# Numerators of a linear attention as 56-by-32 products, features padded to 64, row maxima gathered in columns

## The chip, the cores and the metric

The kernel runs on one core of one Trainium2 chip. The time is the device time of one execution in microseconds (us); where several executions were timed, it is their median. A profile is one further execution, recorded instruction by instruction; its span runs from its first to its last instruction, and its own device time is a little longer than the span.

The engines are named as in the profile: PE is TensorE's matrix products and PEld its weight loads, DVE is VectorE, ACT is ScalarE, POOL is GpSimd, SP is SyncE, which issues all of the kernel's DMAs here. PSUM is the memory that products are written to, in banks of 512 float32 per partition. L507 is line 507 of the kernel.

## What is computed

Two attentions over the same 2048 tokens of 448 features, 16 heads of 28, mixed by a gate per token. The first (A) is linear: queries and keys go through a small matrix per head, then through two softmaxes over 28 values each, and only sums over the tokens are needed. The second (B) is an ordinary softmax attention.

```python
def _A_ref(x, wqkv, w_phi, wo):
    q, k, v = ...                                   # 16 heads of 28
    pq = jnp.einsum("bhsd,hdf->bhsf", q, w_phi)
    pk = jnp.einsum("bhsd,hdf->bhsf", k, w_phi)
    phi_q = jnp.concatenate([_softmax(pq, axis=-1), _softmax(-pq, axis=-1)], axis=-1)
    phi_k = jnp.concatenate([_softmax(pk, axis=-1), _softmax(-pk, axis=-1)], axis=-1)
    kv = jnp.einsum("bhsf,bhsd->bhfd", phi_k, v)    # 56 x 28 per head
    z  = jnp.einsum("bhsf->bhf", phi_k)
    num = jnp.einsum("bhqf,bhfd->bhqd", phi_q, kv)
    den = jnp.einsum("bhqf,bhf->bhq", phi_q, z)[..., None] + 1e-6
    return (num / den) @ wo                         # heads side by side

def _B_ref(x, wqkv, wo):
    scores = jnp.einsum("bhqd,bhkd->bhqk", q, k) * scale
    return (_softmax(scores, axis=-1) @ v) @ wo     # heads side by side

g = _sigmoid((x * gate_w).sum(-1, keepdims=True))
out = g * _A_ref(...) + (1 - g) * _B_ref(...)
```

All inputs and the output are float32.

## The kernel before, in words

The order of the instructions on PE, DVE, ACT and POOL is the order of the program text, written out by hand; the DMAs on SP are ordered by the framework's scheduler, each waiting for its semaphores, and one that waits holds back those behind it.

**Stages.** First the projections to B's queries and keys are computed and kept in DRAM (`proj_qk`). Then comes a loop of 43 rounds (line 681) in which a round i handles key tile t = i and query tile q = i - 16 of attention A, 128 tokens each. Then follow B's values (`value_b`), and from line 1104 on B's attention: 256 steps s, sixteen key tiles for each of 16 groups gq (4 groups of heads by 4 blocks of 512 queries). In a step, `scores` computes 4 heads' scores (line 830), `exps_of` their exponentials on ACT (line 838), and `values` two steps later the products with the values (line 975).

**Features of A.** The weights of A's queries are multiplied by the per-head matrix beforehand (`fold`). For a tile, a product of 448 columns gives pq; `features1` copies it out of PSUM on ACT, takes maximum and minimum per head on DVE (lines 417, 418), subtracts them on POOL (line 420) and on POOL or DVE (line 422, by the argument `eng`), and puts the exponential on ACT's list (line 424). `features2`, called for the tile before, sums (line 431), inverts and scales on POOL (line 433). A tile of features is 16 heads by 2 softmaxes by 28, 896 values per token; it rotates through four buffers, which also hold the last four loads of x before the loop (`load_last`).

**Keys.** `kv_add` adds the products of key features and values to the bank pkv: head 4g + j has its 32 rows (28 values, a one for the sum z, padding) at partitions 32j and its 56 columns at 56g. At round q = 2 `kv_copy` copies pkv out with each 56 columns doubled, at q = 3 `kv_out` turns the copy with four products and multiplies it with a mask, so that KV holds eight blocks of 112 rows by 64 columns, each with two heads on its diagonal.

**Numerators.** `turn` turns a tile's features with eight products, two heads (112 columns) in each, and ACT copies them to fT, 112 partitions by 8 pairs of heads by 256 tokens (two tiles). `numer` multiplies eight times a block of KV with a pair's fT:

```python
for g in range(NG):
    for hh in range(2):
        n = 2 * g + hh
        nc.tensor.matmul(pn[g // 2][64 * hh:64 * hh + 64, g % 2 * 256:g % 2 * 256 + 256],
                         KV[:, n, :], fT_of[tb][:, n, :], start=True, stop=True,
                         tile_position=(0, 64 * hh))
```

`tile_position` gives the row and the column of the array at which the product's weights lie. `normalize1` copies the two banks pn out on ACT and sends the denominators, one row of each 32, by DMA through DRAM to all rows; `normalize2` to `normalize4` divide and split the result into two parts for the output projection `out_a` (line 518), which takes three products for each of four groups of heads. A tile runs through subtraction, turning, numerators and output projection in different rounds (y = q - 1 counts them, lines 727 to 783).

**Row maxima of B.** The exponentials need each query's largest score beforehand, so all scores are computed a second time ahead, with one product and a maximum each. In the first part `mx_unit` does it for groups 0 to 4: four products of 28 rows at four row positions into four banks (line 260), a Relu on ACT and a pass on DVE (line 265); the next unit needs the four banks back. From group 5 on, three such products (line 288) go with every step of B's attention, each reduced on DVE (line 295). The partial maxima lie in `part`. When a group is complete, `mx_reduce` puts a function on the list `fin`, which reduces them to 16 columns of `red` (line 229) and turns `red` in 32-by-32 blocks into a tile `nm` (line 234), of which there are seven buffers. `load_nm` later copies nm's rows into the stack of the group's queries (line 816), four DMAs of 2 KB, where the score products subtract them; the stack alternates between two buffers. In the loop of steps, `load_q(gq + 1)` is called at step 5 of group gq, `load_nm(gq + 1)` at step 12 (at step 14 for group 14), and that of group 15 as soon as its maxima are there.

Of the kernel before, what the change touches and what calls it, by code (L numbers as in the profile page):

```python
# [17 lines left out]
P = 128  # L18
# [18 lines left out]
def f32(ap):  # L37
    return ap.bitcast(F32)
# [3 lines left out]
def gated_mix_kernel(ctx, tc, xT, wqkB, wvB, wvA, wkAT, wqAT, phi, woA, woB,  # L42
# [180 lines left out]
    def mx_reduce(gq):  # L223

        col = 64 * gq
        n = 2 if gq < GM else 4

        def reduce():
            nc.vector.tensor_reduce(
                red.rearrange("p (t c) -> p t c", t=4)[:, :, :4],  # L230
                part[:, col:col + 16 * n].rearrange("p (k t h) -> p t h k", t=4, h=4),
                AX.X, ALU.max)
            nm_of[gq] = nm = mxp.tile([P, 128], F32, tag="nm", name=f"nm{gq}", bufs=7)
            nc.vector.transpose(nm, f32(red))

        mxs["fin"].append(reduce)

# [80 lines left out]

    def load_last(b):

        raw = bd.tile([P, H, 2, DH], F32, tag="feat", name=f"xraw3_{b}", bufs=4)
        raw = raw.rearrange("p h s f -> p (h s f)")[:, :512]
        nc.sync.dma_start(raw, xT[:, b, 1536:])
        return raw

# [43 lines left out]
    def normalize1(pool, pn, nm, n):  # L369

# [41 lines left out]
    def features1(pp, nm, eng):  # L412

        pc = bd.tile([P, H, DH], F32, tag="pc", name=f"pc{nm}", bufs=2)
        nc.scalar.copy(pc, pp[:, :D].rearrange("p (h f) -> p h f", f=DH))
        ext = bd.tile([P, 2, H], F32, tag="ext", name=f"ext{nm}", bufs=3)
        nc.vector.tensor_reduce(ext[:, 0, :], pc, AX.X, ALU.max)
        nc.vector.tensor_reduce(ext[:, 1, :], pc, AX.X, ALU.min)
        f = bd.tile([P, H, 2, DH], F32, tag="feat", name=f"feat{nm}", bufs=4)
        nc.gpsimd.tensor_sub(f[:, :, 0, :], pc,  # L420
                             ext[:, 0, :].unsqueeze(2).to_broadcast([P, H, DH]))
        eng.tensor_sub(f[:, :, 1, :],
                             ext[:, 1, :].unsqueeze(2).to_broadcast([P, H, DH]), pc)
        exps.append(lambda: nc.scalar.activation(f, f, AF.Exp))
        return f

    def features2(f, nm):

        f2 = f.rearrange("p h s f -> p (h s) f")
        sm = bd.tile([P, 2 * H], F32, tag="fsum", name=f"fsum{nm}", bufs=3)  # L430
        nc.vector.tensor_reduce(sm, f2, AX.X, ALU.add)
        nc.vector.reciprocal(sm, sm)
        nc.gpsimd.tensor_mul(f2, f2, sm.unsqueeze(2).to_broadcast([P, 2 * H, DH]))
        return f.rearrange("p h s f -> p (h s f)")

    exps = []

# [6 lines left out]
    def kv_add(t):  # L444

        pf, pvv = fk.pop(t), va.pop(t)
        for g in range(NG):
            for j in range(4):
                h = 4 * g + j
                nc.tensor.matmul(pkv[32 * j:32 * j + 32, g * 56:(g + 1) * 56], pvv[:, h, :],  # L450
                                 pf[:, h * 56:(h + 1) * 56], start=t == 0 and g == 0,
                                 stop=t == NT - 1, tile_position=(0, 32 * j),
                                 skip_group_check=True)

# [14 lines left out]
    def kv_copy():  # L469

        kvT = ta.tile([P, D], F32, tag="ga", name="kvT", bufs=2)
        nc.scalar.copy(
            kvT.rearrange("p (g i f) -> p g i f", i=2, f=56),
            pkv[:, :224].rearrange("p (g f) -> p g f", f=56).unsqueeze(2).to_broadcast([P, NG, 2, 56]))
        return kvT

    def kv_out(kvT):

        pt = ps_s("pkvT")
        for g in range(NG):  # L480
            nc.tensor.transpose(pt[:112, g * P:(g + 1) * P], kvT[:, g * 112:(g + 1) * 112], ident)
        nc.vector.tensor_mul(KV, pt[:112].rearrange("p (n c) -> p n c", c=64),
                             mask_s.unsqueeze(1).to_broadcast([112, 8, 64]))

    def turn(u):

        tb, tl = divmod(u, 2)
        if tl == 0:
            fT_of[tb] = ta.tile([112, 8, 256], F32, tag="fT", name=f"fT{tb}", bufs=1)
        f = fq.pop(u)  # L490
        cut = (0, 4, 8) if u < NT - 2 else (0, 3, 6, 8)
        pt = [ps_s(f"pft{u}_{i}") for i in cut[:-1]]
        for a, b, p in zip(cut, cut[1:], pt):
            for n in range(a, b):
                nc.tensor.transpose(p[:112, (n - a) * P:(n - a + 1) * P],  # L495
                                    f[:, n * 112:(n + 1) * 112], ident)
        for a, b, p in zip(cut, cut[1:], pt):
            nc.scalar.copy(fT_of[tb][:, a:b, tl * P:(tl + 1) * P],
                           p[:112, :(b - a) * P].rearrange("p (n q) -> p n q", q=P))

    def numer(tb):

        pn = [ps_s(f"pn{tb}_{i}") for i in range(2)]
        for g in range(NG):
            for hh in range(2):
                n = 2 * g + hh
                nc.tensor.matmul(pn[g // 2][64 * hh:64 * hh + 64, g % 2 * 256:g % 2 * 256 + 256],  # L507
                                 KV[:, n, :], fT_of[tb][:, n, :], start=True, stop=True,
                                 tile_position=(0, 64 * hh))
        num[tb] = normalize1(ta, pn, f"a{tb}", 2)  # L510

    po_of = {}
# [168 lines left out]
    for i in range(2 * NT + 11):  # L681
# [14 lines left out]
        if q == 2:  # L696
# [4 lines left out]
            KV = ta.tile([112, 8, 64], F32, name="KV")  # L701
# [509 lines left out]
```

## Time and profile before

| | us |
|---|---|
| median of 3 runs | 989.11 |
| the runs | 989.56, 989.11, 986.35 |
| the profiled execution's own time | 986.75 |
| its span | 985.0 |
| A's numerators, first to last start | 204.8 to 284.7 |
| B's attention, 256 steps | from about 356 on |

The page of the profile gives each engine's busy time, the chain of work that ended last with its shares by engine and line, and groups of instructions as "line engine operation out<-in shapes xcount | busy, mean ns of one | idle time before them and what ended it". Three further views are used: the chain in order of time and the timeline (start, duration, engine, what, count), and busy times by stretches. A product's end in the trace is modelled, so a duration of a product holds some 0.16 us in which the next has already begun; starts are better for counting.

### The profile page before, as it was taken

To read this page: it belongs to the slowest core of one execution; us is meant where nothing else is said; L and a number is where in the kernel's file an instruction comes from. 1 tells how busy PE (TensorE), PEld (TensorE's weight loads), DVE (VectorE), ACT (ScalarE), POOL (GpSimd) and SP (SyncE) were. 2 spreads that over 40 slices of the span, in tenths; PEclk is the share of its full clock that TensorE was granted. 3 is DMA by queue.
4 is the path that set the end of the run, shared out by engine and by line. 5 is a ranking of instruction groups with operands and counts; after the bars stand their busy time and mean duration, and the time that the engine had idled before them with its cause. 6 is when DMAs were issued, how large, how long until landed. Compare 5 with 4: busy or idle time off the path is not lost.

```text
span 985.0 us, 22282 instructions
## 1 busy us (share of the span) xinstructions
PE 979.2 (99%) x8392; PEld 607.2 (62%) x8392; DVE 728.5 (74%) x1335; ACT 752.9 (76%) x1442; POOL 234.8 (24%) x224
## 2 busy tenths in 40 slices
PE   9999999999999999999999999999999999999998
PEld 8877877887777665555555555555555555555555
DVE  5566767899766678888888888888888888885112
ACT  4455655577775689988988988988888898897561
POOL 1135535578734710031011001011001011000010
PEclk9999999999999999999999999999999999999999
DMA  9873010013233233121132121122231223000451
GB/s 304 310 253 116 33 54 32 36 37 98 79 103 112 90 114 127 37 58 46 65 89 73 35 61 48 57 82 71 61 83 50 60 58 84 22 20 31 132 159 57
DMA packets 56140, 84.47 MB, mean 86 GB/s; under 512 B 17217, under 2 KB 23985, under 8 KB 56033
## 3 DMA queue, kind: packets, MB, share of 16 engines
q1 hardware_dynamic: 56032, 83.06, 27.3%
q8 instruction: 66, 1.08, 0.5%
q14 instruction: 42, 0.34, 0.1%
HBM read 54.86 MB, written 27.78 MB: 84 GB/s over the span
## 4 chain that ended last, share of the span: by engine, by line
PE 95%; DVE 3%; issue 1%; ACT 0%; POOL 0%; DVEq 0%; POOLq 0%; ACTq 0%
PE g L830 29%; PE pv L975 26%; PE pqk L109 6%; PE poa L109 4%; PE pk L127 4%; PE pva L127 4%; PE g L288 3%; PE pmd L260 3%; PE pob L109 3%; PE pvb L127 2%; PE pvb L109 2%; PE pq L109 2%; PE pn L507 1%; PE pqk L608 1%; PE pft L495 1%
## 5 line engine op out<-in xcount | busy, mean ns | idle before, releaser
L838 ACT ACTIVATE p<-g 128x512 f32<-128x512 f32 x1020 | 526.1, 607 | 83.9 <-PE g L830 83.1
L295 DVE TENSOR_REDUCE part<-g 128x1 f32<-128x512 f32 x704 | 442.3, 684 | 84.4 <-PE g L288 80.4
L830 PEld LDWEIGHTS g<-qst,kst 32*128 32x128 f32 x3060 | 221.2, 183 | 212.1 <-DVE part L295 194.6
L830 PE MATMUL g<-qst,kst 32*128 32x512 f32 x3060 | 337.9, 420 | 0.1
L975 PE MATMUL pv<-p,vb 128*32 128x512 f32 x2048 | 273.0, 605 | 0.0
L288 PE MATMUL g<-kc,qc 28*128 28x512 f32 x704 | 233.3, 495 | 0.0
L394 POOL TENSOR_TENSOR oUb<-oUb,rsb 128x512 f32<-128x512 f32 x15 | 19.3, 1286 | 490.5 <-DMA rsb<-rdb 458.4
L265 DVE CUSTOM_DVE_ANT_0 rl<-pmb,rl 128x512 f32<-128x512 f32 x160 | 103.2, 682 | 44.0 <-ACT rl L264 44.0
L264 ACT ACTIVATE rl<-pmd 128x512 f32<-128x512 f32 x160 | 87.3, 601 | 31.2 <-PE pmb L260 30.0
L288 PEld LDWEIGHTS g<-kc,qc 28*128 28x128 f32 x704 | 86.5, 182 | 0.2
L975 PEld LDWEIGHTS pv<-p,vb 128*32 128x32 f32 x2048 | 40.7, 108 | 65.9 <-issue 64.6
L109 PE MATMUL pqk<-XH,wB 128*128 128x512 f32 x192 | 59.1, 397 | 0.0
L986 DVE SCALAR_TENSOR_TENSOR acc<-pob,gate,acc 128x448 f32<-128x448 f32 x12 | 8.2, 684 | 54.7 <-PE pob L109 54.7
L546 ACT CAST ev<-pqk 128x512 fp32r<-128x512 f32 x28 | 16.0, 589 | 39.5 <-PE pqk L109 23.0
L109 PE MATMUL poa<-woA_s,oTa 128*128 128x448 f32 x192 | 43.5, 375 | 0.0
L260 PE MATMUL pmb<-kp,qp 28*128 28x512 f32 x160 | 42.1, 496 | 0.4
L547 DVE TENSOR_TENSOR ev<-pqk,ev 128x512 fp32r<-128x512 f32 x28 | 19.0, 690 | 30.9 <-ACT ev L546 30.8
L109 PEld LDWEIGHTS pqk<-XH,wB 128*128 128x128 f32 x192 | 35.5, 188 | 8.5 <-issue 1.5
L260 PE MATMUL pmd<-kp,qp 28*128 28x512 f32 x160 | 39.9, 494 | 0.0
L127 PE MATMUL pk<-wkA_s,XH 128*128 128x448 f32 x128 | 39.4, 382 | 0.0
L109 PEld LDWEIGHTS poa<-woA_s,oTa 128*128 128x128 f32 x192 | 35.0, 189 | 6.3 <-issue 2.9
L127 PE MATMUL pva<-wvA_s,XH 128*128 128x450 f32 x128 | 37.8, 372 | 0.0
(154 smaller groups left out, 1089.2 us busy)
## 6 DMA issues: line engine op xcount, KB each, us to landing
qkd<-ev SPq DMA_DIRECT2D x28, 512.0 KB
qst<-qkd SPq DMA_DIRECT2D x64, 112.0 KB
kst<-qkd SPq DMA_DIRECT2D x64, 112.0 KB
od<-oTb SPq DMA_DIRECT2D x48, 112.0 KB
rsa<-rda SPq DMA_DIRECT2D x8, 512.0 KB
oL<-od SPq DMA_DIRECT2D x8, 512.0 KB
rsb<-rdb SPq DMA_DIRECT2D x15, 256.0 KB
gad<-ga SPq DMA_DIRECT2D x16, 224.0 KB
```

What stands on the lines that cost most here:

```text
L109: nc.tensor.matmul(dst, l, r, start=i == 0, stop=i == len(todo) - 1)
L127: nc.tensor.matmul(dst[:, :n], l, r, start=i == 0, stop=i == len(todo) - 1, skip_group_check=True)
L260: nc.tensor.matmul(pm[j], qc[js, qt * P:(qt + 1) * P], kc[js, :], start=True, stop=True, tile_position=(32 * i, 0))
L264: nc.scalar.activation(rl, pm[i], AF.Relu)
L265: nc.vector.tensor_tensor_reduce(rl, pm[2 + i], rl, 1.0, LOWEST, ALU.add, ALU.max, part[:, col + i:col + i + 1])
L288: nc.tensor.matmul(pm, mxs[("qc", gq)][js, qt * P:(qt + 1) * P], mxs[("kc", gq // NQ, kb)][js, :], start=True, stop=True, tile_position=(3 ...
L295: nc.vector.tensor_reduce(part[:, col:col + 1], pm, AX.X, ALU.max)
L394: (nc.gpsimd if n == 1 else nc.vector).tensor_mul(oU, oU, rs)
L547: nc.vector.tensor_sub(e[:, 1, :], pq, f32(e[:, 0, :]))
L830: nc.tensor.matmul(st[j], kst_of[(gq // NQ, kt // 4)][js, k, (kt % 4) * P:(kt % 4 + 1) * P], qst_of[gq][js, q, :], start=n == 0, stop=n == ...
L838: nc.scalar.activation(p, st[j], AF.Exp, scale=SCALE)
L975: nc.tensor.matmul(pv[32 * j:32 * j + 32, :], vb[kt // 8][:, kt % 8, 4 * g + j, :], pt[j], start=kt == 0, stop=kt == NT - 1, tile_position ...
```

## The change

It touches two parts. In attention A, a head's features take 64 columns instead of 56, the last eight unused; the order of the query heads in a tile is permuted, by writing the folded weights `wqA_s` in another order, so that the pair turned together is head 4(2k) + j and head 4(2k + 1) + j. Two turned heads then lie at partitions 0 to 55 and 64 to 119 of fT. KV becomes two blocks of 128 by 128 without zero blocks, so the mask is no longer applied; `kv_copy` no longer doubles columns and clears the padding, `kv_out` turns two blocks instead of four and copies. The numerators are sixteen products of 56 rows by 32 columns, at two row positions and four column positions, the two row positions into two banks; each still has 256 moving columns. Their results lie in another order, which `out_a` follows. The subtraction of line 422 goes to POOL for q = 2. The padding of the four feature buffers is cleared on POOL, for the loads of x that use them first.

For the row maxima, the reduction of group gq writes columns 4(gq % 8) to 4(gq % 8) + 3 of each 32 of `red`; the turn is done in `load_nm`, into one of two buffers, and the rows that belong to the group are loaded from it.

```diff
         n = 2 if gq < GM else 4
+        r = 4 * (gq % 8)
 
         def reduce():
             nc.vector.tensor_reduce(
-                red.rearrange("p (t c) -> p t c", t=4)[:, :, :4],
+                red.rearrange("p (t c) -> p t c", t=4)[:, :, r:r + 4],
                 part[:, col:col + 16 * n].rearrange("p (k t h) -> p t h k", t=4, h=4),
                 AX.X, ALU.max)
-            nm_of[gq] = nm = mxp.tile([P, 128], F32, tag="nm", name=f"nm{gq}", bufs=7)
-            nc.vector.transpose(nm, f32(red))
+            nm_of[gq] = True
...
-        raw = bd.tile([P, H, 2, DH], F32, tag="feat", name=f"xraw3_{b}", bufs=4)
-        raw = raw.rearrange("p h s f -> p (h s f)")[:, :512]
+        raw = bd.tile([P, H, 64], F32, tag="feat", name=f"xraw3_{b}", bufs=4)
+        nc.gpsimd.memset(raw[:, 8:, 56:], 0.0)
+        raw = raw.rearrange("p h f -> p (h f)")[:, :512]
...
-        nc.scalar.copy(dst[:, 0, bs, gs], pw3)
-        nc.vector.tensor_sub(dst[:, 1, bs, gs], pw3, f32(dst[:, 0, bs, gs]))
+        hi, lo = dst[:, 0, bs, gs], dst[:, 1, bs, gs]
+        if nm == "q":
+            pw3 = pw3.rearrange("p b (j f) -> p b j f", f=DH)
+            hi, lo = [dst[:, i, bs, g // 2 * 224:g // 2 * 224 + 224].rearrange(
+                "p b (j e f) -> p b j e f", e=2, f=DH)[:, :, :, g % 2, :] for i in range(2)]
+        nc.scalar.copy(hi, pw3)
+        nc.vector.tensor_sub(lo, pw3, f32(hi))
...
-        f = bd.tile([P, H, 2, DH], F32, tag="feat", name=f"feat{nm}", bufs=4)
+        fw = bd.tile([P, H, 64], F32, tag="feat", name=f"feat{nm}", bufs=4)
+        f = fw[:, :, :2 * DH].rearrange("p h (s f) -> p h s f", s=2)
...
-        exps.append(lambda: nc.scalar.activation(f, f, AF.Exp))
+        fe = fw[:, :, :2 * DH]
+        exps.append(lambda: nc.scalar.activation(fe, fe, AF.Exp))
...
-        nc.gpsimd.tensor_mul(f2, f2, sm.unsqueeze(2).to_broadcast([P, 2 * H, DH]))
+        nc.gpsimd.tensor_mul(f, f, sm.unsqueeze(3).to_broadcast([P, H, 2, DH]))
...
-        nc.scalar.copy(
-            kvT.rearrange("p (g i f) -> p g i f", i=2, f=56),
-            pkv[:, :224].rearrange("p (g f) -> p g f", f=56).unsqueeze(2).to_broadcast([P, NG, 2, 56]))
+        kvw = kvT[:, :256].rearrange("p (g f) -> p g f", f=64)
+        nc.vector.memset(kvw[:, :, 56:], 0.0)
+        nc.scalar.copy(kvw[:, :, :56],
+                       pkv[:, :224].rearrange("p (g f) -> p g f", f=56))
...
-        for g in range(NG):
-            nc.tensor.transpose(pt[:112, g * P:(g + 1) * P], kvT[:, g * 112:(g + 1) * 112], ident)
-        nc.vector.tensor_mul(KV, pt[:112].rearrange("p (n c) -> p n c", c=64),
-                             mask_s.unsqueeze(1).to_broadcast([112, 8, 64]))
+        for k in range(2):
+            nc.tensor.transpose(pt[:, k * P:(k + 1) * P], kvT[:, k * P:(k + 1) * P], ident)
+        nc.vector.tensor_copy(KV, pt[:, :256].rearrange("p (k c) -> p k c", c=P))
...
-                nc.tensor.transpose(p[:112, (n - a) * P:(n - a + 1) * P],
-                                    f[:, n * 112:(n + 1) * 112], ident)
+                nc.tensor.transpose(p[:, (n - a) * P:(n - a + 1) * P],
+                                    f[:, 2 * n:2 * n + 2].rearrange("p e c -> p (e c)"), ident)
...
-        for g in range(NG):
-            for hh in range(2):
-                n = 2 * g + hh
-                nc.tensor.matmul(pn[g // 2][64 * hh:64 * hh + 64, g % 2 * 256:g % 2 * 256 + 256],
-                                 KV[:, n, :], fT_of[tb][:, n, :], start=True, stop=True,
-                                 tile_position=(0, 64 * hh))
+        for k in range(2):
+            for j in range(4):
+                for e in range(2):
+                    es = slice(64 * e, 64 * e + 2 * DH)
+                    nc.tensor.matmul(pn[e][32 * j:32 * j + 32, k * 256:(k + 1) * 256],
+                                     KV[es, k, 32 * j:32 * j + 32], fT_of[tb][es, 4 * k + j, :],
+                                     start=True, stop=True, tile_position=(64 * e, 32 * j))
...
-                        for x in out_passes(oTs[tb][g // 2], g % 2 * 256 + tl * P, woA_s[:, :, :, :D], g)])
+                        for x in out_passes(oTs[tb][g % 2], g // 2 * 256 + tl * P, woA_s[:, :, :, :D], g)])
...
-            fq[q] = features1(pq, f"q{q}", nc.vector if 0 < q < 9 else nc.gpsimd)
+            fq[q] = features1(pq, f"q{q}", nc.vector if q in (1, 3, 4, 5, 6, 7, 8) else nc.gpsimd)
...
-        nm = nm_of.pop(gq)
+        nm_of.pop(gq)
+        r = 4 * (gq % 8)
+        nm = mxp.tile([P, 128], F32, tag="nm", name=f"nm{gq}", bufs=2)
+        nc.vector.transpose(nm, f32(red))
...
-            nc.sync.dma_start(row[:, :, b, :], nm[32 * b:32 * b + 4, :].rearrange("h (t r) -> h t r", t=4))
+            nc.sync.dma_start(row[:, :, b, :], nm[32 * b + r:32 * b + r + 4, :].rearrange("h (t r) -> h t r", t=4))
```

More of the change, by code (lines that the diff above doesn't have):

```diff
@@ L423, in features1, with features2 @@
                              ext[:, 1, :].unsqueeze(2).to_broadcast([P, H, DH]), pc)
-        exps.append(lambda: nc.scalar.activation(f, f, AF.Exp))
[L425 to L431, printed above, removed]
+        fe = fw[:, :, :2 * DH]
+        exps.append(lambda: nc.scalar.activation(fe, fe, AF.Exp))
+        return fw
+    def features2(fw, nm):
+        f = fw[:, :, :2 * DH].rearrange("p h (s f) -> p h s f", s=2)
+        sm = bd.tile([P, H, 2], F32, tag="fsum", name=f"fsum{nm}", bufs=3)
+        nc.vector.tensor_reduce(sm, f, AX.X, ALU.add)
         nc.vector.reciprocal(sm, sm)
-        nc.gpsimd.tensor_mul(f2, f2, sm.unsqueeze(2).to_broadcast([P, 2 * H, DH]))
-        return f.rearrange("p h s f -> p (h s f)")
+        nc.gpsimd.tensor_mul(f, f, sm.unsqueeze(3).to_broadcast([P, H, 2, DH]))
+        return fw
     exps = []
@@ L450, in kv_add @@
                 nc.tensor.matmul(pkv[32 * j:32 * j + 32, g * 56:(g + 1) * 56], pvv[:, h, :],
-                                 pf[:, h * 56:(h + 1) * 56], start=t == 0 and g == 0,
+                                 pf[:, h, :2 * DH], start=t == 0 and g == 0,
                                  stop=t == NT - 1, tile_position=(0, 32 * j),
@@ L488, in turn @@
         if tl == 0:
-            fT_of[tb] = ta.tile([112, 8, 256], F32, tag="fT", name=f"fT{tb}", bufs=1)
+            fT_of[tb] = ta.tile([P, 8, 256], F32, tag="fT", name=f"fT{tb}", bufs=1)
         f = fq.pop(u)
@@ L494, in turn @@
             for n in range(a, b):
-                nc.tensor.transpose(p[:112, (n - a) * P:(n - a + 1) * P],
-                                    f[:, n * 112:(n + 1) * 112], ident)
+                nc.tensor.transpose(p[:, (n - a) * P:(n - a + 1) * P],
+                                    f[:, 2 * n:2 * n + 2].rearrange("p e c -> p (e c)"), ident)
         for a, b, p in zip(cut, cut[1:], pt):
             nc.scalar.copy(fT_of[tb][:, a:b, tl * P:(tl + 1) * P],
-                           p[:112, :(b - a) * P].rearrange("p (n q) -> p n q", q=P))
+                           p[:, :(b - a) * P].rearrange("p (n q) -> p n q", q=P))
     def numer(tb):
         pn = [ps_s(f"pn{tb}_{i}") for i in range(2)]
-        for g in range(NG):
-            for hh in range(2):
-                n = 2 * g + hh
-                nc.tensor.matmul(pn[g // 2][64 * hh:64 * hh + 64, g % 2 * 256:g % 2 * 256 + 256],
-                                 KV[:, n, :], fT_of[tb][:, n, :], start=True, stop=True,
-                                 tile_position=(0, 64 * hh))
+        for k in range(2):
[5 more added lines that the diff above has]
+                                     start=True, stop=True, tile_position=(64 * e, 32 * j))
         num[tb] = normalize1(ta, pn, f"a{tb}", 2)
@@ L700, in gated_mix_kernel @@
             stg = ta_s.enter_context(tc.tile_pool(name="stg", bufs=2, reuse_waits="tile"))
-            KV = ta.tile([112, 8, 64], F32, name="KV")
+            KV = ta.tile([P, 2, P], F32, name="KV")
             kvT = kv_copy()
```

## The prediction

> **What bounds the kernel now.** I read the page's head and its share of the chain of waits first, then busy time by stretches, and then the chain inside the stretch that the change touches.
>
> ```profile
> span 985.0 us, 22282 instructions
> ...
> PE 95%; DVE 3%; issue 1%; ACT 0%; POOL 0%; DVEq 0%; POOLq 0%; ACTq 0%
> ```
>
> The chain that ended last is TensorE nearly throughout. Two parts that the change touches are found by tile, with shortest, median and longest duration and first and last start:
>
> ```profile
> L507 PE MATMUL pn<-fT,KV x128: 378/379/432, 204.8 to 284.7; 112*64 112x256 f32 x128
> ...
> L234 DVE STREAM_TRANSPOSE nm<-red x16: 311/311/313, 111.6 to 900.1; 128x128 f32<-128x128 f32 x16
> ```
>
> The numerators are confined to 205 to 285 us, the turns of the row maxima are spread over the whole run. By stretches (length, then busy time of PE, weight loads, DVE, ACT, POOL, then clock, DMA share, GB/s):
>
> ```profile
> 193.00:205.00 12.00, 11.98 (x92) 10.49 (x82) 11.55 (x23) 7.61 (x14) 6.27 (x5) 1.00 0.12 46
> 205.00:225.00 20.00, 19.66 (x130) 15.00 (x130) 19.34 (x34) 15.75 (x29) 15.15 (x11) 1.00 0.25 66
> 225.00:245.00 20.00, 20.00 (x127) 16.26 (x124) 17.80 (x35) 15.77 (x30) 19.17 (x16) 1.00 0.27 83
> 245.00:265.00 20.00, 20.00 (x124) 15.72 (x123) 14.36 (x30) 14.46 (x26) 15.07 (x12) 1.00 0.23 71
> ```
>
> Up to 225 us VectorE is as full as TensorE (19.34 of 20). From 225 on only TensorE is full, with GpSimd close to it (19.17) until 245. The chain shows the change of hands, and then one period of the second regime:
>
> ```profile
> 198.01 1.22 DVE featq L422
> ...
> 222.50 0.60 DVE rl L265
> ...
> 223.16 0.49 PE pmb L260
> 223.66 1.88 PE pn L507 x16
> ...
> 232.47 0.43 PE pmd L260 x2
> ...
> 247.17 1.88 PE pn L507 x16
> 249.05 2.66 PE poa L109 x12
> 251.70 0.87 PE pft L495 x8
> ```
>
> Until 223.1 the chain runs in VectorE; at 223.16 a score product starts when VectorE's pass over the previous unit gives back its bank, and from there product follows product with no gap. So before 223 us a TensorE saving shows only as far as VectorE is also sooner; after it, microsecond for microsecond.
>
> **The numerators.** One pair of token tiles takes 1.88 us, and there are eight pairs: 15 us in all.
>
> ```profile
> L507 PE MATMUL pn<-fT,KV 112*64 112x256 f32 x128 | 15.6, 386 | 0.0
> ...
> 232.84 0.44 PE L507 MATMUL pn<-fT,KV 112*64 112x256 f32 x2
> ...
> 232.84 0.65 PE L507 MATMUL pn<-fT,KV 112*64 112x256 f32 x4
> ```
>
> 128 records for 64 products: each leaves two records. In the timeline two records together span 0.44 us and four span 0.65 us, so the second pair adds 0.21: two records run side by side, one in each half of the columns, and a round lasts 0.215 us. Sixteen records are eight rounds, 8 x 0.215 = 1.72, and 0.16 of filling and draining makes the 1.88. The change makes it 32 records of 56 rows by 32 columns with the same 256 moving columns. If all eight places of the array work at once, that is four rounds, 0.86, plus the 0.16, plus 0.05 until the eighth has started: 1.07, a saving of 0.81. No row of this trace has halves of the rows and quarters of the columns in one product. The nearest rows are the key-value products, with four places side by side:
>
> ```profile
> 192.31 0.26 PE L450 MATMUL pkv<-featk,vap 128*32 128x56 f32 x4
> ...
> 192.31 0.30 PE L450 MATMUL pkv<-featk,vap 128*32 128x56 f32 x8
> ```
>
> Four records of four heads span 0.26 us and eight span 0.30: the next four cost only 0.05, so four quarters of the columns do run together and their weight loads hide. Row quarters do it too: the four 28-row products of line 260 take 0.43 us (row 232.47), where the output products of 448 columns take 2.66 / 12 = 0.22 each in turn. From these bounds a numerator group costs between 1.07 (eight at once) and 1.88 (four at once: 32 records in eight rounds, no gain); if only two went together it would be 16 rounds, 3.60. I take 1.07, since both ways of dividing are seen to work and the eight write two banks, one for each half of the rows.
>
> A rule speaks against it. The Trainium skill (TensorE: The Clock Gate, "Packing small matmuls — row/col tiling") says that matmuls start and end strictly in program order, and its table there gives nine tiles 6.32 times and sixteen 10.6 times, about 0.68 of the ideal. By that share the eight would be worth 5.4, a group 32 x 0.215 / 5.4 + 0.16 = 1.43, and the gain little over half of mine. By strict order the two records of one product could not be passed by the next head's; the key-value rows, where four start within 0.05 us, disagree with that.
>
> Where it counts: eight groups start from 204.8 us on, the third at 223.66, so the first two fall under VectorE's time. The third is followed at 232.47 by a score product that needs the bank VectorE ends reading in this row:
>
> ```profile
> 231.16 0.69 DVE L265 CUSTOM_DVE_ANT_0 rl<-pmb,rl 128x512 f32<-128x512 f32 x1
> ```
>
> 231.85 against 232.47: 0.62 of the third 0.81 is free. The other five count in full, 5 x 0.81 = 4.05. Together 4.67 us.
>
> **VectorE before 223 us.** Removed there are one feature subtraction (q = 2, given to GpSimd) and the masking of KV; added are a small memset and a 256-column copy.
>
> ```profile
> L422 DVE TENSOR_TENSOR featq<-extq,pcq 128x448 f32<-128x448 f32 x8 | 8.6, 1071 | 0.8
> L422 POOL TENSOR_TENSOR featq<-extq,pcq 128x448 f32<-128x448 f32 x8 | 7.6, 944 | 0.0
> ...
> L482 DVE TENSOR_TENSOR KV<-pkvT,mask_s 112x512 f32<-112x512 f32 x1 | 0.7, 678 | 0.0
> ...
> L163 DVE MEMSET red<- 128x128 f32 x1 | 0.2, 165 | 0.8 <-PEq L1198 0.8
> ...
> 198.14 0.53 ACT L415 COPY pcq<-pq 128x448 f32<-128x448 f32 x1 [1.74 <-PE pq L109]
> ```
>
> On paper 1.22 (the instance at 198.01) + 0.68 - 0.35 (half of the 0.68) - 0.16 = 1.4 us less. But the next tile's minima wait for the copy that ScalarE ends at 198.67, itself waiting for TensorE, so VectorE starts them 0.5 sooner, not 1.2; and the exponential of q = 2 then waits for GpSimd's 0.94, behind its two subtractions of line 420, so VectorE's next sum comes only some 0.25 us sooner. I take 0.25, from bounds 0 and 1.4. GpSimd has the room: 6.27 busy of 12.
>
> **Turning the features.** 112 columns per product become 128. The nearest row for 128 columns of float32 is line 1072:
>
> ```profile
> L495 PE MATMUL pft<-ident,featq 128*112 128x128 f32 x128 | 17.1, 276 | 0.0
> ...
> L1072 PE MATMUL pr<-ident,rw 128*128 128x128 f32 x8 | 1.2, 288 | 0.0
> ```
>
> 17.1 / 128 = 0.134 each against 1.2 / 8 = 0.150, so between 0 and 128 x 0.016 = 2.1 us in all; much of the second is one group's filling, and I take 0.3. kv_out has two products instead of four, 0.2 us less, under VectorE's time.
>
> **Features in rows of 64.** Exponential, sum and scaling keep 896 elements per row but in runs of 56 with gaps. Rows with and without gaps:
>
> ```profile
> L415 ACT COPY pcq<-pq 128x448 f32<-128x448 f32 x16 | 8.6, 536 | 12.9 <-PE pq L109 12.9
> L459 ACT COPY vap<-pva 128x448 f32<-128x448 f32 x16 | 8.6, 535 | 4.0 <-PE pva L127 4.0
> ...
> L433 POOL TENSOR_TENSOR featq<-featq,fsumq 128x896 f32<-128x896 f32 x16 | 31.9, 1993 | 16.8 <-DVE fsumq L432 14.2 <-DVE dena L382 2.7
> ...
> L420 POOL TENSOR_TENSOR featk<-pck,extk 128x448 f32<-128x448 f32 x16 | 15.1, 943 | 60.8 <-DVE extk L417 60.8
> ```
>
> ScalarE copies 448 elements into runs of 28 with gaps (line 459) as fast as without. On GpSimd the gapped 448 of line 420 cost 0.943, twice that is 1.89, no more than the 1.99 of line 433. So 0, with up to 0.2 per tile on GpSimd, hidden by its waits except between 225 and 245. The four memsets of line 322 fall in GpSimd's idle time at the start and the loads do not wait for them: 0. The strided copies of the folded weights have the same element counts: 0.
>
> **The row maxima.** Sixteen turns of 0.31 us stay sixteen. Before, a turn follows its reduction and the 2 KB loads go out long ahead; now the turn is in load_nm, four steps before the stack is used (two for group 14), with the loads behind it on SP.
>
> ```profile
> 865.62 1.89 DVE L295 TENSOR_REDUCE part<-g 128x1 f32<-128x512 f32 x3 [0.36 <-PE g L288]
> 867.96 1.89 DVE L295 TENSOR_REDUCE part<-g 128x1 f32<-128x512 f32 x3 [0.46 <-PE g L288]
> ...
> 871.96 0.50 PE L830 MATMUL g<-qst,kst 32*128 32x512 f32 x2
> ...
> 899.81 0.26 DVE L229 TENSOR_REDUCE red<-part 128x16 fp32r<-128x64 f32 x1
> 900.10 0.31 DVE L234 STREAM_TRANSPOSE nm<-red 128x128 f32<-128x128 f32 x1
> ...
> 903.40:903.80 0.40, 0.40 (x4) 0.38 (x3) 0.00 (x0) 0.00 (x0) 0.00 (x0) 1.00 0.04 5
> 903.80:904.80 1.00, 1.00 (x15) 0.54 (x13) 0.54 (x1) 0.00 (x0) 0.00 (x0) 1.00 0.00 0
> ```
>
> VectorE idles 0.46 us before the next step's reductions, so a turn of 0.31 fits the gap, where today's reduction and turn together, 0.57, do not. Group 15 shows the path: turned at 900.10, DMA quiet from 903.80, 3.7 us. For group 14 the turn would come at 867.5 and land at 871.2; its first scores start at 871.96. It holds by 0.75 us; the others have two steps, 4.6 us, more. Behind the waiting loads on SP stand key and query stacks due twelve steps later or more, and the group's denominators, which are copied out only after its end. So 0, from -0.5 to +1.
>
> **Sum.** The profiled execution took 986.75 us: 985.0 of span and 1.75 around it. -4.67 - 0.25 + 0.3 = -4.6, which gives 982.1 on its basis. It lies low among the runs (986.35, 989.11, 989.56); from the middle of these ends, 988.0, the sum gives 983.4, which I predict.
>
> **Rivals.** (1) Four places at once: the halves of the rows take turns, or TensorE does not look far enough ahead past the second records of seven other products. For it: no row shows the combination. Against it: each way of dividing works alone. Gain 0.25 - 0.3: 988. (2) Strict order: the second record of a product runs beside the first of the next, never more than two together. Sixteen products make 17 rounds, 17 x 0.215 + 0.16 = 3.8 per group, 1.9 more; eight groups, TensorE being full in all their stretches: 15 us, 1003, slower. The key-value rows speak against it. This is what the rule of the Trainium skill above would do. (3) The row maxima come late: slower once a turn and its loads take over 4.5 us for group 14, or over 9 for the rest; at 1 us for each of 15 groups, 15 us on the forecast, 998. The 3.7 us path speaks against it. (4) GpSimd becomes the bound from 225 to 245, where it has 0.83 us free: if gaps make each scaling a third longer than 1.99, five tiles there ask 3.3 and 2.5 of it is lost: 986. The gapped row of line 420 speaks against it.
>
> **How the numbers follow.** Eight at once 0.66 (983.4, itself 980 to 986), rival 1 0.15, rival 2 0.06, rival 3 0.06, rival 4 0.07. The range 979.5 to 989.5 takes in bounds of 0 to 2.1 on the turning, 0 to 1.4 on VectorE and rivals 1 and 4, and leaves out 2 and 3. A measurement of this kernel can tell 0.3%, 3 us: faster has the forecast and a part of rival 4, 0.68; the same is rival 1 and the rest, 0.19; slower 0.13.
>
> **What would show it.** Right: in the chain, numerators of about 1.07 us per group with 32 records, turning still near 0.9 to 1.0 per tile, and the first score product some 4.5 us sooner, with the step of 2.3 us after it unchanged. Wrong: numerator groups of 1.4 us or more, GpSimd without idle time past 245 us, or TensorE waiting for qst at a change of group. The forecast falls first if eight places do not run at once.

## The result, and the profile after

The changed kernel took 1012.89 us in the median of four runs (1011.9 to 1015.75), beside 987.73 before: a ratio of 1.0268, 95% interval 1.0254 to 1.0281. It is slower by 2.7%, where 983.4 us was predicted. The profiled execution took 1011.9 us, with a span 25.1 us longer than before. The page after, its head, the chain's share by engine, and one group:

```profile
span 1010.1 us, 22531 instructions
...
PE 82%; DMA 7%; DVE 5%; SPq 2%; issue 2%; POOL 1%; ACT 1%; DVEq 0%; POOLq 0%; ACTq 0%
...
L845 PE MATMUL g<-qst,kst 32*128 32x512 f32 x3060 | 338.7, 421 | 19.7 <-DMA qst<-nm 19.4
```

TensorE's share of the chain fell from 95% to 82%, and transfers now hold 7%. The score products (L830 before, L845 now) stood idle 19.4 us for `qst<-nm`, the load of the row maxima. On the page before they stood idle 0.1 us in all:

```profile
L830 PE MATMUL g<-qst,kst 32*128 32x512 f32 x3060 | 337.9, 420 | 0.1
```

The numerators did what was predicted. From the chain after, the third and the seventh group:

```profile
224.37 1.13 PE pn L519 x32
...
270.66 1.02 PE pn L519 x32
```

32 records in 1.02 us (1.07 predicted, 1.88 before): all eight places work at once. The turning of the features did not grow either. By tile, with the shortest, median and longest duration, first and last start:

```profile
L506 PE MATMUL pft<-ident,featq x128: 271/273/331, 199.0 to 276.4; 128*128 128x128 f32 x128
L519 PE MATMUL pn<-fT,KV x256: 376/376/401, 206.4 to 282.5; 56*32 56x256 f32 x128
```

The median of 273 ns for a turning record is that of before (112 columns, 270/273/325).

To see where the 25.1 us lie, three marks are taken from both profiles: the first and the last sum of keys and values that stand in the chain, and the first value products of the attention stage in PE's timeline. The chain before:

```profile
93.93 0.92 PE pkv L450 x64
...
180.38 0.92 PE pkv L450 x64
```

and after:

```profile
95.15 0.92 PE pkv L461 x64
...
181.33 0.93 PE pkv L461 x64
```

PE's timeline before:

```profile
362.25 1.07 PE L975 MATMUL pv<-p,vb 128*32 128x512 f32 x8
```

and after:

```profile
364.08 1.06 PE L990 MATMUL pv<-p,vb 128*32 128x512 f32 x8
```

| stretch, us | before | after | difference |
|---|---|---|---|
| to the first sum of keys and values | 93.93 | 95.15 | +1.22 |
| from there to the last | 86.45 | 86.18 | -0.27 |
| from there to the attention stage | 181.87 | 182.75 | +0.88 |
| attention stage, to the end of the span | 622.75 | 646.02 | +23.27 |

The first line is no effect: two experiments below whose program is the same in that stretch reach the mark at 93.84 (od_pool) and 96.84 (nm_early). The third should have read -4.6. The fourth is the loss.

**The attention stage.** A step of 2.3 us stays one, but at ten of the changes to the next group of 16 steps TensorE stands still. (`od` are the stores of B's results, `woB` the weights of B's output projection.) SP's timeline after, for the change to the third group (group 2), with the turn on VectorE and the product that waits:

```profile
423.42 0.86 SPq L1047 DMA_DIRECT2D od<-oTb  x1
425.15 1.90 SPq L973 DMA_DIRECT2D woB_raw<-in_woB_dram  x5
427.09 2.52 SPq L1047 DMA_DIRECT2D od<-oTb  x3
...
430.65 2.38 SPq L831 DMA_DIRECT2D qst<-nm  x4
...
422.62 0.30 DVE L828 STREAM_TRANSPOSE nm<-red 128x128 f32<-128x128 f32 x1
...
434.20 0.50 PE L845 MATMUL g<-qst,kst 32*128 32x512 f32 x2 [2.46 <-DMA qst<-nm]
```

The maxima are turned at 422.9, but their loads go out at 430.65, 7.7 us later, because SP first waits for the previous group's `od` stores (until 423.42, when GpSimd has made oTb) and then issues six loads of weights and the other three stores; the sixth weight load again waits for GpSimd, until 430.2. Before, the same loads stood right behind the query stack and ahead of all of that:

```profile
391.73 3.48 SPq L804 DMA_DIRECT2D qst<-qkd  x4
395.26 2.37 SPq L816 DMA_DIRECT2D qst<-nm  x4
...
421.49 0.87 SPq L1032 DMA_DIRECT2D od<-oTb  x1
```

A second price follows the wait. By stretches around the change to group 7 (length, then busy time of PE, weight loads, DVE, ACT, POOL, then clock, DMA share, GB/s):

```profile
622.00:627.00 5.00, 1.97 (x24) 0.83 (x22) 1.69 (x3) 2.12 (x5) 0.00 (x0) 1.00 0.21 54
627.00:634.00 7.00, 7.00 (x65) 2.95 (x61) 5.14 (x9) 4.54 (x9) 0.00 (x0) 0.76 0.18 66
```

After TensorE has stood for 3 of 5 us its clock is 0.76 over the next 7 us, 0.24 x 7 = 1.7 us lost. The Trainium skill (TensorE: Matmul & The Clock Gate, "What's actually happening") says that an idle window of about 3.4 us halves the clock until a busy window has passed; half the clock for 3.4 us is the same 1.7, so the price in this row agrees. The condition does not: TensorE never stood for a whole 3.4 us. In the trace's clock records the half clock comes for 3.41 us each after the stalls of 1.91, 3.04 and 2.64 us that end at 511.1, 626.6 and 667.7, and not after one of 2.71 us that ends at 861.0. Three times 1.7 us, with the 19.4 us of waiting, make 24.5, close to the stage's 23.3.

**The first stage.** (`dena` are the loads of the denominators, `rsa` the load that brings their reciprocals back to all rows, `gad` the stores of A's gated result.) Up to the eighth numerators the changed kernel had gained; then VectorE waits 6.4 us. The timelines of VectorE and SP after:

```profile
277.79 2.06 DVE L144 TENSOR_TENSOR wvB_s<-wvB_raw,wvB_s 128x896 fp32r<-128x896 f32 x1
286.28 0.18 DVE L391 TENSOR_SCALAR dena<-dena 128x32 f32<-128x32 f32 x1 [6.43 <-DMA qp<-qkd]
...
276.01 0.57 SPq L385 DMA_DIRECT2D dena<-oUa  x1
276.68 0.54 SPq L397 DMA_DIRECT2D rsa<-rda  x1
277.32 0.54 SPq L385 DMA_DIRECT2D dena<-oUa  x1
```

In the chain the second dena load stands with the time until it landed:

```profile
277.32 8.39 DMA dena<-oUa
```

And the stretch that follows:

```profile
290.00:310.00 20.00, 20.00 (x99) 15.14 (x97) 10.41 (x29) 11.55 (x22) 8.47 (x7) 0.92 0.38 116
```

The timelines of the same place before:

```profile
279.15 2.06 DVE L144 TENSOR_TENSOR wvB_s<-wvB_raw,wvB_s 128x896 fp32r<-128x896 f32 x1
281.13 1.73 DVE L382 TENSOR_SCALAR dena<-dena 128x32 f32<-128x32 f32 x1
...
276.11 1.16 SPq L376 DMA_DIRECT2D dena<-oUa  x2
277.36 0.53 SPq L388 DMA_DIRECT2D rsa<-rda  x1
```

The timeline names qp as what VectorE waited for, but the chain has the second dena load, which lands 8.39 us after its issue. Before, both dena loads went ahead of the 512 KB of rsa; now the second stands behind them. The semaphore records of the trace show why this costs so much: rsa itself, issued at 276.68, has its last four arrivals at 284.53 to 285.53, and the second dena load has four at 284.72 to 285.71. Of the sixteen arrivals of the gad store issued next, at 277.95, twelve come by 279.94 and four at 285.23 to 286.18. So it looks as if rsa and dena run on the same four of the core's sixteen DMA engines, and only what lies on these four waits for rsa. VectorE also comes 1.36 us sooner, so it only waits longer: dena's operation ends at 286.46 in place of 282.86, 3.6 us later. The clock of 290 to 310 us is 0.92, where before it was 1.00 throughout: 1.6 us more.

### The profile page after: what moved, and what is told of

It is laid out like the page before. It is cut to its first block, busy times and chain, and to the rows that moved or that the text cites. A ratio compares the mean times of both kernels' runs of the same rounds, so it can differ in the third digit from the quotient of the medians.

```text
span 1010.1 us, 22531 instructions
## 1 busy us (share of the span) xinstructions
PE 980.4 (97%) x8518; PEld 600.7 (59%) x8518; DVE 723.8 (72%) x1335; ACT 753.0 (75%) x1442; POOL 236.6 (23%) x229
## 4 chain that ended last, share of the span: by engine, by line
PE 82%; DMA 7%; DVE 5%; SPq 2%; issue 2%; POOL 1%; ACT 1%; DVEq 0%; POOLq 0%; ACTq 0%
PE g L845 26%; PE pv L990 24%; PE pk L127 4%; PE pva L127 4%; PE pqk L109 3%; PE g L288 3%; PE poa L109 3%; PE pob L109 3%; PE pmd L260 3%; PE pvb L127 2%; DMA qkd<-ev 2%; PE pvb L109 2%; DMA qst<-nm 2%; SPq L831 1%; PE pq L109 1%
## 5 line engine op out<-in xcount | busy, mean ns | idle before, releaser
L845 PEld LDWEIGHTS g<-qst,kst 32*128 32x128 f32 x3060 | 219.7, 184 | 236.2 <-DVE part L295 189.1
L845 PE MATMUL g<-qst,kst 32*128 32x512 f32 x3060 | 338.7, 421 | 19.7 <-DMA qst<-nm 19.4
L109 PE MATMUL pq<-wqA_s,XH 128*128 128x448 f32 x128 | 37.4, 374 | 0.6 <-ACT oUa L382 0.6
```

The lines of the kernel that those rows point to most:

```text
L109: nc.tensor.matmul(dst, l, r, start=i == 0, stop=i == len(todo) - 1)
L845: nc.tensor.matmul(st[j], kst_of[(gq // NQ, kt // 4)][js, k, (kt % 4) * P:(kt % 4 + 1) * P], qst_of[gq][js, q, :], start=n == 0, stop=n == ...
```

## The experiments

The theory, Q: the attention stage lost because the turn, asked for later, moved the four loads behind the od stores in SP's order. Rival F: the padded features and the numerators cost it. For the first stage, D: the dena load behind rsa.

**max_only.** The kernel before, with the row-maxima part alone.

```diff
-                red.rearrange("p (t c) -> p t c", t=4)[:, :, :4],
+                red.rearrange("p (t c) -> p t c", t=4)[:, :, r:r + 4],
...
-            nm_of[gq] = nm = mxp.tile([P, 128], F32, tag="nm", name=f"nm{gq}", bufs=7)
-            nc.vector.transpose(nm, f32(red))
...
-        nm = nm_of.pop(gq)
+        nm_of.pop(gq)
+        r = 4 * (gq % 8)
+        nm = mxp.tile([P, 128], F32, tag="nm", name=f"nm{gq}", bufs=2)
+        nc.vector.transpose(nm, f32(red))
```

> The kernel before with the row-maxima part of the change alone: reductions write their columns, the turn and its tile come when the stack is loaded (step 12 of the group); features and numerators as before. Theory Q (the four row-maxima loads now stand on SP's queue behind the group's four od stores, so that at ten of the fifteen changes of group the scores wait for them): the whole loss of the attention stage comes along, 646.0 less 622.8, 23.3 us: 987.7 + 23.3 = 1011. Rival F (the loss comes from the padded features and the numerators of eight tiles, through the clock or the transfers): 988, within 3.

1014.2 us beside 986.76 before, 1.0266 (1.0247 to 1.0286). The whole loss is there without the numerators. In PE's list of waits (us in total, times, longest):

```profile
PE g L833 <- DMA qst<-nm: 20.6, 10, 2.8
```

Ten waits again. F falls.

**nm_early.** The changed kernel, asking for the turn six steps sooner.

```diff
-            if kt == (12 if gq + 1 < 14 else 14) and gq + 1 < NG * NQ - 1:
+            if kt == (6 if gq + 1 < 14 else 10) and gq + 1 < NG * NQ - 1:
```

> The changed kernel with the turn and the four loads asked for at step 6 of a group (10 for the fourteenth) in place of 12 and 14; nothing else. Theory Q: in SP's order the loads then stand behind the query stack and ahead of the od stores, the attention stage falls back to 622.8 us, the first stage keeps its stall at 277 to 286 us: 1012.9 - 23.3 = 989.6. Rival F: 1013. Rival T (the turn finds its reductions late on VectorE wherever it is asked for): 1013 or more.

988.39 us, 1.0016 (1.0005 to 1.0026) of before: 24.5 us of the loss are gone. SP's timeline, as far as the od stores:

```profile
411.60 2.36 SPq L831 DMA_DIRECT2D qst<-nm  x4
...
426.46 0.87 SPq L1047 DMA_DIRECT2D od<-oTb  x1
```

The loads are out 15 us before the first od, and no wait for them is left. This alone doesn't say whether the time of the turn or SP's order counted. That is the next run.

**od_pool.** The turn stays at step 12; the od stores leave SP.

```diff
-                nc.sync.dma_start(o_d[r:r + DH, :, qb * 512:(qb + 1) * 512],
+                nc.gpsimd.dma_start(o_d[r:r + DH, :, qb * 512:(qb + 1) * 512],
```

> The changed kernel with the od stores issued from GpSimd's queue in place of SP's; the turn and the row-maxima loads stay at step 12, on SP. Theory Q (SP's order is what makes the loads late): nothing that waits stands ahead of them, they are issued within 1 us after the turn, 989.6, up to 2 more if GpSimd's stores are slow. Rival L (the turn at step 12 is itself too late for the first scores of the next group): 1013.

1002.13 us, 1.0155 (1.0132 to 1.0178): between the two, so neither number held. The list of waits:

```profile
PE g L845 <- DMA qst<-nm: 9.2, 3, 4.3
```

SP's timeline at two of the three that are left:

```profile
429.07 0.35 SPq L132 DMA_DIRECT2D woB_raw<-in_woB_dram  x1
429.48 2.37 SPq L831 DMA_DIRECT2D qst<-nm  x4
...
728.34 0.41 SPq L959 DMA_DIRECT2D oL<-od  x1
728.80 2.49 SPq L831 DMA_DIRECT2D qst<-nm  x4
```

Seven of ten waits are gone with the turn where it was, so step 12 was not too late, and rival L falls. In the three that stay, another load stands ahead of the maxima and holds SP: a load of weights that goes out only at 429.07, and loads of oL, which read what the od stores have just written. Q holds in a wider form: not od, but whatever waits ahead on SP.

**max_early.** max_only with the line of nm_early.

> The kernel before with the row-maxima part alone, as max_only, but the turn and its loads asked for at step 6 (10 for the fourteenth group). Theory Q: the whole 25 to 28 us of max_only go, 987 within 1.5. If gathering the maxima as columns costs by itself (tiles of red that wait for each other, the turn on VectorE in the attention stage): 989 or more.

985.96 us beside 986.3, 0.9994 (0.9985 to 1.0003). Gathering the maxima as columns costs nothing that shows once its loads keep their place.

**both.** nm_early with the sixteen dena loads of the first stage issued from ScalarE.

```diff
-            nc.sync.dma_start(den[:, i, :], oU[DH:P:32, i, :])
+            (nc.scalar if n == 2 else nc.sync).dma_start(den[:, i, :], oU[DH:P:32, i, :])
```

> As nm_early, and the sixteen loads of the first stage's denominators (dena) issued from ScalarE's queue in place of SP's. Theory D (in the changed kernel's order on SP the second of the two dena loads at 277 us comes after the 512 KB of rsa and lands 8.4 us later; before, both came ahead of it): the stall goes, and with it 1.8 us of loss and in its place the 4.6 us of gain that the numerators give: 989.6 - 6.4 = 983.2. Rival (the stall has another cause, or ScalarE pays as much for the issues): 989.6 or above, and the wait of VectorE on dena stays at 6 us.

984.68 us, 0.9980 (0.9967 to 0.9993): 3.7 us less than nm_early, and 1.5 us of the expected gain are missing. Of VectorE's waits for dena the longest is 3.0:

```profile
DVE dena L391 <- DMA dena<-oUa: 3.3, 2, 3.0
```

But ScalarE's timeline has a place where it now stands at its own loads, two of which take it 0.55 us each elsewhere:

```profile
227.56 4.42 ACTq L385 DMA_DIRECT2D dena<-oUa  x2
```

Its next copy (232.02) had waited 4.01 us. The 9 us at 222 us that the next expectation speaks of are not in this trace.

**both_a6.** Only the two dena loads of the pair that stalled leave SP.

```diff
-            nc.sync.dma_start(den[:, i, :], oU[DH:P:32, i, :])
+            (nc.scalar if nm in ('a6',) else nc.sync).dma_start(den[:, i, :], oU[DH:P:32, i, :])
```

> As nm_early, and of the sixteen dena loads only the two of the seventh pair of tiles (the pair of the stall) are issued from ScalarE; the other fourteen stay on SP. Theory D2 (in the run 'both' ScalarE stood 9 us at its own dena load of 222 us, behind a load of wvB; with that gone the numerators' gain reaches the end): counted from the first sum of keys and values, the seven gaps of the numerators gave 2.3 us and their last 0.86 by 283 us, so 986.8 - 0.3 - 3.2 = 983.3, and the wait of VectorE on dena at 277 is under 2 us. By the prediction's sum, 982. Rival (what the numerators save is used up before the attention stage whatever is done to dena): 986 to 988.

984.94 us beside 986.3, 0.9988 (0.9977 to 0.9998). It lies 3.45 us below nm_early (2.8 by the two ratios) with two loads moved, and VectorE no longer waits for dena there; this is D. But 983.3 was not reached: the time lies between the expectation and its rival. The chain shows what limits next:

```profile
277.06 8.97 DMA gad<-ga
...
287.58 8.72 DMA dena<-oUa
```

SP's timeline just ahead of them:

```profile
276.46 0.56 SPq L397 DMA_DIRECT2D rsa<-rda  x1
...
286.98 0.55 SPq L397 DMA_DIRECT2D rsa<-rda  x1
```

Both are issued right behind an rsa, and both land some 9 us later. This lateness is not new: before, the gad store behind rsa was issued at 277.99 and had its last arrival at 286.29, but nothing in the chain waited for it. Before, the chain from 262 to 292 us was TensorE alone.

**num_twice.** both_a6 with each numerator product issued twice (`for k in (0, 1, 0, 1)`).

> As both_a6, with every one of the 256 numerator products issued twice into the same places. If the 1.02 us of a group's numerators lies wholly on the path: 8 x 1.02 = 8.2 us above both_a6. By the prediction's count of groups on the path (5 in full, 0.62 of one, two under VectorE): 5.7. If other engines set the pace there: under 3.

990.19 us, 5.25 above both_a6. A group in its chain:

```profile
236.82 1.89 PE pn L519 x64
```

1.89 us, 0.87 more, so 5.25 / (8 x 0.87) = 0.75 of the added time reaches the end. The prediction's sum, 4.67 of 8 x 0.81, is 0.72. (The expectation took the 0.62 us of the third group for a share of a group.) That the two shares are close is luck. In the profiles the seven gaps between the starts of the groups grew by 0.4, 0.4, 3.5, 0.0, 0.9, 0.5 and 0.4 us; the 3.5 hold a new wait of VectorE (3.4 us) for a load of denominators, which stands in the chain:

```profile
219.53 9.13 DMA dena<-oUa
```

SP's order had changed again: here an rsa (218.23) goes out ahead of both dena loads, in both_a6 (217.42) behind them. So this run does not confirm the count by groups, and shows D at another place.

**num_same.** both_a6 with the loops in the order j, e, k, so that two products of one place follow each other.

> As both_a6, with the numerators' loops turned so that the two products of one place follow each other at once (j, half, k) in place of going round all eight places. If a place works through its own queue while the records behind it start at other places: 1.02 us a group, the time of both_a6. If records start strictly in their order in the program: each pair serial, about 1.9 us a group, 5 us above both_a6.

984.84 us, that of both_a6 within the interval. In its chain:

```profile
233.56 1.35 PE pn L519 x32
248.83 1.07 PE pn L519 x32
```

Five of the eight groups took 1.07, three 1.32 to 1.35, against 1.02 to 1.13 before the turn of the loops. So a product that must wait for its place does not hold back those for other places. The Trainium skill (TensorE: Matmul & The Clock Gate, "The mechanism") has matmuls start and end in strict order. Strict starts would have let the second product of a place begin only after the first's two rounds of 0.215 us, and the next place only after that: at least 8 x 0.43 = 3.4 us (the expectation's 1.9 is too low). These rows contradict that for the starts.

**q29_act.** both_a6 with one GpSimd subtraction fewer for query tiles 2 and 9: the second half of their features is the negated tile without its minimum.

```diff
+        if nm in ("q2", "q9"):
+            nc.scalar.activation(f[:, :, 1, :], pc, AF.Copy, scale=-1.0)
```

> As both_a6, with one GpSimd subtraction (0.9 us) taken away for query tiles 2 and 9: their second half of features is a copy of the negated tile on ScalarE, without its minimum, which the later division by the sum takes out again. Theory P (from 225 us GpSimd sets the pace: its three featq operations and the split oTa end at 234.7 us, 2.1 us after the fourth numerators, so the fourth gap is 14.5 us where PE's work is 13.4): the fourth gap falls by about 0.9 to 13.6 us, the first numerators start about 0.5 us sooner, 983.9 at the end. Rival V (VectorE is as full there, 12.9 of 13 us, and takes over): gap and time stay, 984.9.

984.93 us, no change. The first numerators start 0.9 us sooner after the first sum of keys and values (110.35 against 111.25), but the fourth gap is 14.47. Its chain there:

```profile
235.19 1.15 ACT rl L264 x2
236.34 1.29 POOL oTa L412
```

GpSimd's oTa now follows ScalarE's work, which stands in the chain ahead of it. The edit had itself given ScalarE a copy for each of the two tiles. Rival V's numbers held, but the chain names ScalarE where V named VectorE. P falls as it was put: 0.9 us less on GpSimd alone did not shorten the gap.

**gad_act.** both_a6 with the gad stores issued from ScalarE (`nc.scalar.dma_start(ga_d[...`).

> As both_a6, with the sixteen gad stores issued from ScalarE's queue in place of SP's. Theory R (what is issued on SP right behind a 512-KB rsa lands 9 us later; the store of 277 us held its buffer so long that ScalarE waited 2.1 us for it at 286): the store lands in under 5 us, the wait goes, 1 to 2 us off both_a6, 983.4. Rival (all queues share the same transfers and the store is as late from any): 984.9 or, with 16 issues of 0.45 us on ScalarE, up to 987.

992.5 us, 1.0061 (1.0047 to 1.0074): worse than both ends. ScalarE's timeline:

```profile
296.32 1.08 ACT L264 ACTIVATE rl<-pmd 128x512 f32<-128x512 f32 x2 [3.69 <-DMA rsa<-rda]
```

ScalarE stood until rsa had landed before it could issue a store, and its exponentials and copies with it. By the trace the store at 295.89 first waits for semaphore 104, which it is to use itself and which the rsa load of 285.97 still held; that load's last arrival was at 295.82. The stores themselves did land sooner: the one issued at 286.39, 0.4 us behind this rsa, had its last arrival at 292.48, after 6.1 us, where both_a6's took 8.97. That is still more than the 5 us expected, and the price on ScalarE was higher than the gain.

## Why the prediction was wrong, point by point

**The row maxima are the step that failed.** It read: "Behind the waiting loads on SP stand key and query stacks due twelve steps later or more, and the group's denominators, which are copied out only after its end. So 0, from -0.5 to +1." That looked at what stands behind the loads, and at the path from turn to landing (3.7 us), as if SP were free when the turn ends. It didn't look at what stands ahead of them. With the turn at step 12 the scheduled order of SP has the loads behind the od stores, though on the chip the turn of group 2 ended (422.92) half a microsecond before the first store went out (423.42): once the order is fixed, being ready first is of no use. The price was 23.3 us in the trace, 24.5 in nm_early's times, 27 in max_only's (1014.2 - 986.76), whose profile has six stretches of 3.41 us at half clock in the attention stage in place of three. Group 14, on which the step spent its sum, was not among the ten. The sign was named, TensorE waiting for qst at a change of group, but without a price from the queue.

**Rival 3 was the right kind**, with a chance of 0.06 and 998 us. Its bound from turn to landing was right, as od_pool shows, but it had no term for the queue.

**Numerators: right in mechanism and size.** 1.02 to 1.13 us a group against 1.07; rivals 1 and 2 fall. The gaps between the starts of successive groups, from PE's timeline: before 8.75, 9.99, 9.25, 14.26, 14.25, 9.75, 12.02; after 7.84, 10.11, 8.75, 14.52, 13.42, 9.59, 11.19. They sum to 2.85 less, and the last group is 0.86 shorter. The first group starts 0.55 later from the last sum of keys and values in the chain, so by the end of the eighth 3.2 us were won of the 4.67.

**Which groups count was off.** The first saves 0.91 though it was counted as hidden. The fourth, counted in full, saves nothing (14.52 against 14.26); PE waits there, 0.6 us for GpSimd's oTa. The chain after, where the chain before had only products:

```profile
229.37 2.04 POOL featq L444
...
234.87 1.30 POOL oTa L412
...
236.21 1.69 PE poa L109 x7
```

That is rival 4's place, 225 to 245, though its reason is wrong: the scaling of features in rows of 64 takes no longer (median 1.71 us both times). From 225.5 to 236.2 the chain runs through VectorE and then GpSimd, whose work TensorE's longer numerators had just covered.

**VectorE before 223 us**: the third numerators start 0.24 us sooner after the last sum of keys and values in the chain (42.97 against 43.21), 0.25 predicted. That is luck. The first numerators start 0.55 later, so the stretch ahead of them grew where it was to shrink, and the next two gaps, whose shorter numerators the prediction counted as hidden, won 0.79. q = 2's subtraction, which the change gave to GpSimd, is a cause: with it taken from GpSimd (q29_act) the first numerators start 0.9 us sooner.

**Turning**: 0.3 taken; the median record did not grow. **Rows of 64 and memsets**: 0 holds for the scaling (1.71 us); the memsets were not tested by themselves.

**After the last numerators** the prediction let the gain reach the end. From the end of the eighth group (285.00 before, 282.79 after) to the attention stage it takes 77.25 us before and 81.29 after, 4.0 us given back to transfers and the clock. That term is missing in the sum. With two loads moved (both_a6) it is 78.27, still 1.0 more. So of the 4.6 us about 1.4 reach the end in both_a6's times (0.2 to 2.3 by its interval). That what is missing there lies in the transfers behind rsa is read from its chain only; gad_act, which moved a store, brought ScalarE's wait in its place, so it stays open.

## What to carry to other kernels

When a load is made ready later, price its place in the queue and not only its own path: list what waits ahead of it on the issuing engine, and when each of those is released. A cheap move of the request (here one number, step 6 for step 12) can be worth more than the change itself: 24.5 us, against about 1.4 from the numerators. A saving on the bounding engine counts group by group only as far as the other engines and the transfers of that stretch are also ahead.

## What the runs showed of the hardware

Eight products of 56 rows by 32 columns run side by side: 32 records of 376 ns each, about 12 us of records, took 1.02 us in the changed kernel's order of issue and 1.07 to 1.35 in the other order tried. Transfers issued on SP right behind the 512 KB of rsa took 8.3 to 9.1 us to land in the cases read here, dena's 8 KB (8.39, 8.72, 9.13) as long as gad's 224 KB (8.97), of which twelve of sixteen arrivals came within some 2 us. The Trainium skill (DMA: Bandwidth & Descriptors, "Queues, rings and completion order") says that each DMA engine takes a ring's descriptors in their order, which agrees. ScalarE as an issuer of transfers can be held at the issue, 4.4 us for two loads in both and 3.69 us in gad_act, with all its computing behind it; in gad_act it waited for the semaphore that an earlier, unrelated load still held.
